# Shifted copies of V by block on GpSimd and VectorE, and a first product taken input by input: one change at the start of a Trainium2 kernel

## The chip, the cores and the metric

The kernel runs on one core of one Trainium2 chip. The time is the device time of one execution in microseconds (us), and smaller is better. A core has TensorE (PE in the profile, with its weight loads as PEld), VectorE (DVE), ScalarE (ACT), GpSimd (POOL) and SyncE (SP), an on-chip memory SBUF, an accumulation memory PSUM that TensorE writes, and 16 DMA engines. Each engine works through its own list of instructions in order. DMAs are issued by an engine, here mostly by POOL, and then run on their own.

## The reference

Sliding-window causal attention (8 batches, 8 heads, 576 positions, head size 64, window 64), followed by a two-layer feed-forward stage with a hard-swish between.

```python
rel = pos[:, None] - pos[None, :]
mask = (rel >= 0) & (rel < 64)
scores = np.where(mask, scale * np.matmul(q, k.transpose(0, 1, 3, 2)), -1e9)
attn = softmax(scores)                      # over the keys
x = np.matmul(attn, v)                      # then to (8*576, 512): 4608 tokens
h = x @ w_in                                # 512 -> 2048
g = h * np.clip(h + 3.0, 0.0, 6.0) / 6.0
out = g @ w_out                             # 2048 -> 512
```

Inputs and output are float32; the kernel computes in bfloat16 with float32 accumulation.

## The kernel before

**Tiling.** Heads go in pairs: a unit of attention is t = 4 * batch + pair, so T = 32 units. The feed-forward stage works on blocks of TB = 512 tokens, nine in all. Of a block, the first product gives 16 tiles hT of 128 features by 512 tokens (index fc), each the sum of four products, one for each pair of heads (`g` in L485: input g of the product is `xT[:, g]`). ACT and DVE then turn hT into gT (L494, L495). The second product gives four tiles of 128 tokens by 512 outputs, each the sum of 16 products (L518), in units of four.

**Order.** The order of instructions on each engine is the order of the program text; nothing is reordered (`manual_schedule`). Waits between engines follow from which tiles, and which parts of them, an instruction reads and writes. `moe` is a queue of feed-forward units, and `weave(n)` issues the next n of them among the attention of a later batch.

**Batch 0** has a path of its own. POOL issues its loads: q and k by pair (L107), then V (L126, five blocks of 128 positions, the last of 64), then the input weights in three parts (L163: a quarter, a quarter and a half of the columns, that is fc 0 to 3, 4 to 7 and 8 to 15), then fills that build the masks (`late_windows`, L196), the output weights in two halves (L169), and q, k and V of batch 1 (L118, L137). TensorE begins with products on zeros (`warm`, L656), turns q and k (`t_q`, `t_k`, L221) as they land and computes scores (`s0_`, L248 and L251), which ACT exponentiates.

The window of 64 lies across blocks of 128, so V is also needed shifted by 64 positions. `Vn[0]` holds batch 0's V by block, `Vs[0]` the shifted one: its upper half of block m is the lower half of Vn's block m, and its lower half of block m + 1 is the upper half of Vn's block m. `shift_early(g, move)` (L147) makes it for one pair of heads and all blocks in two copies. DVE does pairs 0 and 1 (L711, L712), ACT pairs 2 and 3 (L714, L715).

`pv_early(t)` (L354) multiplies the weights with Vn and Vs, and DVE divides by the sums (L363, L364) into `opg`. `x_early(t)` turns that on TensorE (L375, into a PSUM tile `xp`) and ACT copies it to `xT` (L378): this is input g of the first product. `begin(0, pools, between)` (L554, called at L726) starts the first product of block 0: for fc 0, 1 and 2 it issues inputs 0 to 2, then `x_early(3)`, then fc 3's inputs 0 to 2, and then input 3 of these four. The other 12 tiles follow from the queue, all four inputs at a time.

**PSUM** has eight banks: ps_t has three, ps_h two, ps_acc one, and ps_o one tile of two. A tile is held until its last reader has read it.

**Batch 1** follows from L775: two units of the second product, the turn of pair 4, two units, and then a loop over the four pairs, which issues the turn of the next pair, the scores and (L790) 2, 4 and 2 units of the second product.

The start of the program, in its order (excerpt):

```python
load_early_v()                                   # L678
for i in range(3):
    load_w_in(i)                                 # L680
late_windows()                                   # L681
load_w_out(0)
...
for g in range(2):
    shift_early(g, nc.vector.tensor_copy)        # L712
s0_(3)
for g in range(2, NG):
    shift_early(g, nc.scalar.copy)               # L715
```

Of the kernel before, what the change touches and what calls it, by code (L numbers as in the profile page):

```python
# [10 lines left out]
F32 = mybir.dt.float32  # L11
# [13 lines left out]
P = 128  # L25
D = 64
W = 64
# [9 lines left out]
def kernel(  # L37
# [9 lines left out]
    nc = tc.nc  # L47
    B, H, S, _ = q.shape
    DM, FF = moe_w_in.shape
    NT = B * S  # L50
    NG = H // 2
    SP = S // R
    NW = S // W
    NM = (S + P - 1) // P
    NFC = FF // P
    TB = 512
# [12 lines left out]
    ps_o = ctx.enter_context(tc.tile_pool(name="ps_o", bufs=1, space=PSUM))  # L69
    ps_t = ctx.enter_context(tc.tile_pool(name="ps_t", bufs=3, space=PSUM))  # L70
    ps_h = ctx.enter_context(tc.tile_pool(name="ps_h", bufs=2, space=PSUM))
    ps_acc = ctx.enter_context(tc.tile_pool(name="ps_acc", bufs=1, space=PSUM))
# [14 lines left out]
    Vn, Vs = ([t[:].rearrange("p (m h c) -> p m h c", m=NM, h=H) for t in Vflat[i::2]] for i in range(2))  # L87
# [56 lines left out]
            memset(t[:, :, :, 0:VO], 1.0)  # L144
            memset(t[:, :, :, VO + P : VW], 1.0)

    def shift_early(g, move):  # L147

        vn, vs = Vn[0], Vs[0]
        hs = slice(2 * g, 2 * g + 2)  # L150
        move(out=vs[W:P, :, hs], in_=vn[0:W, :, hs])
        move(out=vs[0:W, 1:NM, hs], in_=vn[W:P, 0 : NM - 1, hs])

    def shift(b):

# [4 lines left out]
    def load_w_in(i):  # L160
        n = FF // 4
        c = (slice(0, n), slice(n, 2 * n), slice(2 * n, FF))[i]
        nc.gpsimd.dma_start(  # L163
            out=win16[:, :, c], in_=moe_w_in[:, c].rearrange("(g p) f -> p g f", p=P)
        )
# [14 lines left out]
    zeros = consts.tile([P, TB], BF16, name="zeros")  # L180
# [20 lines left out]
    def late_windows():  # L201

        for part in halves:
            select(band, part, -1, 1, -1, 0.0)
            select(band, part, W, -1, 1, 0.0)
            select(first, part, 0, -1, 1, 0.0)
# [29 lines left out]
    def t_k(t):  # L236
        b, g = divmod(t, NG)
        tp = transposed_heads(ps_acc, staged[b][1], g)
        nc.vector.tensor_copy(
            out=KT[t % 4][:, W:].rearrange("q (p r) -> q p r", r=R),  # L240
            in_=tp[:].rearrange("q r p -> q p r"),
        )
# [96 lines left out]
    def pv_early(t):  # L339
        b, g = divmod(t, NG)  # L340
        vn, vs, pz, pl = Vn[b % 2], Vs[b % 2], Pz[t % 4], Pl[t % 4]
        if t in (1, 3):
            os = [ps_h.tile([P, 1, 512], F32, name="oh", tag="bk") for _ in range(2)]
        else:
            os = [ps_o.tile([P, 2, 512], F32, name="o", tag="o")]
        n = len(os)
        for h in range(2):
            hh = 2 * g + h
            o = os[h % n][:, h // n]
            for m in range(NM):  # L350
                om = o[:, m * (D + 1) : (m + 1) * (D + 1)]
                for a in range(2):
                    last = m == NM - 1
                    nc.tensor.matmul(  # L354
                        om[a * W : (a + 1) * W], lhsT=pl[:, h, a * W : (a + 1) * W] if last else pz[:, h, m, a, :],
                        rhs=(vn if a and not last else vs)[:, m, hh, 0 : D + 1], start=True, stop=True,
                    )
        opg = work.tile([P, NM, 2, D], BF16, name="opg")
        for i, o in enumerate(os):
            hs = slice(i, i + 2 // n)  # L360
            ov = o[:, :, 0 : NM * (D + 1)].rearrange("p h (m c) -> p h m c", c=D + 1)
            rec = recs[:, t, hs, 0:NM]
            nc.vector.reciprocal(out=rec.unsqueeze(3), in_=ov[:, :, :, D : D + 1])  # L363
            nc.vector.tensor_tensor(  # L364
                out=opg[:, :, hs].rearrange("p m h d -> p h m d"), in0=ov[:, :, :, 0:D],
                in1=rec.unsqueeze(3).to_broadcast([P, 2 // n, NM, D]), op=MULT,
            )
        opgs[t] = opg

    def x_early(t):  # L370
        b, g = divmod(t, NG)
        opg = opgs.pop(t)
        tp = ps_t.tile([P, NM, P], BF16, name="xp", tag="bk")
        for m in range(NM):
            nc.tensor.transpose(  # L375
                out=tp[:, m, :], in_=opg[:, m].rearrange("p h d -> p (h d)"), identity=ident[:]
            )
        nc.scalar.copy(out=xT[:, g, 0:S], in_=tp[:].rearrange("p m q -> p (m q)")[:, 0:S])  # L378
# [86 lines left out]
    halfway, units = {}, {}  # L465

    def first_units(kb):
        t0 = kb * TB % XR
        gT = gpool.tile([P, NFC, TB], BF16, name="gT")
        gTs[kb] = gT  # L470

        def unit(fc, part=2, pool=None):
            if part < 2 and fc in halfway:
                hT = halfway.pop(fc)
            else:
                if pool is None:
                    if late[0] == 0:
                        pool = (ps_h, ps_h, ps_t, ps_acc, ps_t, ps_t)[(fc - NG) % 6]
                    else:
                        pool = ps_t if late[0] == 1 or fc % 2 else ps_h  # L480
                hT = (
                    ps_o.tile([P, 2, 512], F32, name="hTo", tag="o")[:, 0] if pool is ps_o
                    else pool.tile([P, TB], F32, name="hT", tag="bk")[:]
                )
            for g in ((0, 1, 2), (3,), range(NG))[part]:  # L485
                nc.tensor.matmul(  # L486
                    hT, lhsT=win16[:, g, fc * P : (fc + 1) * P], rhs=xT[:, g, t0 : t0 + TB],
                    start=(g == 0), stop=(g == NG - 1),
                )
            if part == 0:  # L490
                halfway[fc] = hT
                return
            t1 = t1pool.tile([P, TB], BF16, name="t1")
            nc.scalar.activation(out=t1[:], in_=hT, func=RELU, bias=half_const[:], scale=1.0 / 6.0)  # L494
            nc.vector.scalar_tensor_tensor(  # L495
                out=gT[:, fc, :], in0=t1[:], scalar=1.0, in1=hT, op0=MIN, op1=MULT
            )

        units[kb] = unit
        return [lambda fc=fc: unit(fc) for fc in range(NFC)]  # L500
# [30 lines left out]
    moe = deque()  # L531
# [3 lines left out]
    def queue_block(kb, kept=2 * NG):  # L535

        f = first_units(kb)
        moe.extend(left[:2])
        del left[:2]
        n = len(left)  # L540
        for i, unit in enumerate(f):
            moe.extend(left[i * n // NFC : (i + 1) * n // NFC])
            moe.append(unit)
        left[:] = second_units(kb)
        n = len(left) - kept
        moe.extend(left[:n])
        del left[:n]
# [6 lines left out]
    def begin(kb, pools, between):  # L554

        def part(fc):
            moe.popleft()
            units[kb](fc, 0, pools[fc])

        for fc in range(3):  # L560
            part(fc)
        between()
        for fc in range(3, len(pools)):
            part(fc)
        for fc in range(len(pools)):
            units[kb](fc, 1)

    def weave(n):
        for _ in range(min(n, len(moe))):
            moe.popleft()()  # L570
# [82 lines left out]

    T = B * NG

    def warm(pool, n):  # L656

        wt = pool.tile([P, TB], F32, name="wt", tag="bk")
        for _ in range(n):
            nc.tensor.matmul(wt[:], lhsT=zeros[:, 0:P], rhs=zeros[:], start=True, stop=True)  # L660

    nc.vector.memset(zeros[:], 0.0)
    nc.vector.memset(ident[:], 0.0)
# [3 lines left out]
        out=ident[:], in_=ident[:], pattern=[[-1, P]], compare_op=mybir.AluOpType.not_equal,  # L667
# [8 lines left out]
    nc.vector.memset(first[:], 1.0)  # L676
    pads(1, nc.vector.memset)
    load_early_v()  # L678
    for i in range(3):
        load_w_in(i)  # L680
    late_windows()  # L681
    load_w_out(0)
    staged[1] = load_qk(1, 2)
# [3 lines left out]
    nc.vector.memset(recs[:], 1.0)  # L687
    zero_rows(1)
    nc.vector.memset(Pl[0][:], 1.0)
    nc.vector.memset(Vs[0][0:W, 0], 0.0)  # L690
    for t in Pl[1:]:
        nc.vector.memset(t[:], 1.0)
    nc.vector.memset(ones[:], 1.0)
# [2 lines left out]


    warm(ps_h, 12)
    t_k(0)
    t_q(0)  # L700
    t_k(1)
# [6 lines left out]
    t_k(3)  # L708
    t_q(3)
    s0_(2)  # L710
    for g in range(2):  # L711
        shift_early(g, nc.vector.tensor_copy)  # L712
    s0_(3)
    for g in range(2, NG):  # L714
        shift_early(g, nc.scalar.copy)  # L715
    warm(ps_acc, 6)
    pv_early(0)
    pv_early(1)
    warm(ps_acc, 2)
    x_early(0)  # L720
    pv_early(2)
    x_early(1)
    pv_early(3)
    x_early(2)
    queue_block(0, 0)
    begin(0, (ps_acc, ps_t, ps_t, ps_o), lambda: x_early(3))  # L726
    def group(t, n):

        if t >= 2 * NG:
# [35 lines left out]
    n = NG  # L765
# [12 lines left out]
    for t in range(n, n + 4):  # L778
        if t < n + 3:
            turn(t + 1)  # L780
        s = s_first(t, min(t + 1, n + 3))

        def copies():
            if t < n + 3:
                turned(t + 1, 0)
                turned(t + 1, 1)

        weights(t, s, s_rest(t), own, copies)
        if t < n + 3:
            weave((2, 4, 2)[t - n])  # L790
    nc.gpsimd.tensor_copy(out=seen[:], in_=P0[(n + 3) % 4][0:1, 0, 0, 0:1])
    staged[2] = load_qk(2, 1)
    for t in range(n, n + 4):
# [22 lines left out]
    for t in range(2 * NG, T):  # L816
        b, g = divmod(t, NG)
# [52 lines left out]
```

## Time and profile before

| | before |
|---|---|
| median of 3 runs | 324.89 us (324.28 to 325.29) |
| the profiled execution | 324.49 us |
| its span, first to last instruction | 322.8 us |
| TensorE busy | 307.5 us (95%) |
| DVE, ACT, POOL busy | 177.3, 187.4, 122.9 us |
| TensorE busy from 17.13 to 21.78 us | 3.82 of 4.65 us |
| TensorE busy from 21.78 to 25.35 us | 3.19 of 3.57 us |
| TensorE busy from 25.35 to 36.57 us | 11.22 of 11.22 us |

Times inside the profile count from the span's start. "Busy" is the time in which an engine has an instruction under way; waits, DMA issues apart, are not in it. The chain that ended last goes back from the last instruction, at each step to what released it. A timeline line gives start, duration, engine, line, operation, tiles (out<-in) and, in brackets, the idle time before it and what ended that. A line of the DMA view gives the tile, the issuing queue, how many, the size of one and the median time from issue to landing. "L495" is line 495 of the kernel.

### The profile page before, as it was taken

What the parts mean: (1) busy time and instruction counts of PE and PEld (TensorE: products, weight loads), DVE (VectorE), ACT (ScalarE), POOL (GpSimd) and SP (SyncE); (2) the same over time, 40 slices, a digit from 0 to 9 for tenths busy, and PEclk for the clock granted to TensorE, in tenths of its full rate; (3) what the DMA queues carried; (4) which work ended last, traced back from release to release, by engine and by line L of the source; (5) the groups of instructions that cost most, each with busy time, mean ns of one, the idle gap of its engine ahead of it and who ended that gap; (6) DMA issues with size and microseconds to landing.
All of it is one profiled execution on the core that took longest, in us unless ns stands there. A gap on an engine that the chain in (4) does not pass through costs nothing.

```text
span 322.8 us, 11140 instructions
## 1 busy us (share of the span) xinstructions
PE 307.5 (95%) x4822; PEld 155.5 (48%) x4822; DVE 177.3 (55%) x384; ACT 187.4 (58%) x349; POOL 122.9 (38%) x167
## 2 busy tenths in 40 slices
PE   6889999999999999999999999999999999999992
PEld 2744455445444555555555555555544444444440
DVE  7676647488446752775277626762666156334300
ACT  2768565598547764776477637773674256445310
POOL 8961204688775434563356335633331000000000
PEclk9999999999999999999999999999999999999997
DMA  6999994979979942993299338943012200110011
GB/s 92 161 211 207 207 181 110 214 105 115 197 104 164 125 116 88 162 131 111 80 163 129 115 100 139 152 102 94 17 51 52 85 32 0 60 40 34 34 70 69
DMA packets 57592, 35.67 MB, mean 111 GB/s; under 512 B 39872, under 2 KB 51648, under 8 KB 57536
## 3 DMA queue, kind: packets, MB, share of 16 engines
q0 software_dynamic: 35904, 18.81, 44.6%
q1 hardware_dynamic: 21632, 16.08, 19.2%
q8 instruction: 39, 0.64, 0.8%
q14 instruction: 17, 0.14, 0.1%
HBM read 37.62 MB, written 9.44 MB: 146 GB/s over the span
## 4 chain that ended last, share of the span: by engine, by line
PE 83%; DVE 4%; DMA 3%; ACT 3%; POOL 3%; issue 2%; SPq 0%; POOLq 0%; DVEq 0%; ACTq 0%
PE hT L486 36%; PE acc L518 35%; PE o L403 4%; PE s L310 2%; PE acco L518 2%; PE tk L276 2%; DMA V<-in_v_dram 2%; DMA xT<-opg 2%; POOL qk L107 2%; POOL V L126 1%; ACT t L494 1%; DVE gT L495 1%; DVE opg L364 1%; PE tq L276 1%; ACT e L323 0%
## 5 line engine op out<-in xcount | busy, mean ns | idle before, releaser
L495 DVE SCALAR_TENSOR_TENSOR gT<-t,hT 128x512 bf16<-128x512 bf16 x142 | 97.0, 688 | 84.8 <-ACT t L494 84.0
L486 PE MATMUL hT<-xT,win 128*128 128x512 bf16 x568 | 133.9, 379 | 1.7 <-DVE gT L495 0.6
L518 PE MATMUL acc<-wout,gT 128*128 128x512 bf16 x544 | 129.0, 379 | 0.6 <-ACT QZ L283 0.6
L494 ACT ACTIVATE t<-hT,half_const 128x512 bf16<-128x512 f32 x142 | 97.0, 689 | 52.8 <-PE hT L486 52.3
L486 PEld LDWEIGHTS <-win 128*128 128x128 bf16 x576 | 55.7, 98 | 68.4 <-issue 3.4
L518 PEld LDWEIGHTS <-gT 128*128 128x128 bf16 x576 | 54.3, 98 | 63.6 <-issue 0.9
L331 POOL TENSOR_TENSOR Pz<-e,band 128x512 bf16<-128x512 bf16 x48 | 54.2, 1146 | 0.0
L328 POOL TENSOR_TENSOR P<-e,first 64x256 bf16<-64x256 bf16 x24 | 15.9, 663 | 87.4 <-ACT e L319 87.4
L524 ACT COPY osb<-acc 128x512 f32<-128x512 f32 x34 | 19.9, 586 | 42.2 <-PE acc L518 36.2
L323 ACT ACTIVATE e<-s 128x512 bf16<-128x512 f32 x56 | 30.0, 590 | 0.0
L283 DVE COPY KT<-tk 128x576 bf16<-128x576 bf16 x28 | 20.8, 743 | 5.3 <-ACT e L319 4.5
L137 POOL DMA_DIRECT2D V<-in_v_dram x22 | 18.0, 821 | 11.8 <-DMA win<-in_moe_w_in_dram 5.9
L412 DVE TENSOR_REDUCE sums<-o 128x12 f32<-128x24 f32 x26 | 4.6, 178 | 27.4 <-PE o L403 27.4
L403 PEld LDWEIGHTS <-Pz 64*64 64x64 bf16 x1120 | 13.4, 108 | 12.8 <-issue 11.4
L426 DVE TENSOR_TENSOR opl<-o,recs 128x256 bf16<-128x256 f32 x52 | 19.2, 406 | 0.0
L283 ACT COPY QZ<-tq 128x576 bf16<-128x576 bf16 x28 | 17.8, 636 | 1.5 <-PE tq L276 1.5
L319 ACT ACTIVATE e<-tk 64x128 bf16<-64x128 f32 x28 | 7.6, 271 | 14.4 <-PE tq L296 14.4
L403 PE MATMUL o<-V,Pz 64*64 64x65 bf16 x1040 | 15.3, 195 | 0.0
L310 PE MATMUL s<-QZ,KT 64*64 64x64 bf16 x896 | 14.4, 195 | 0.4 <-DVE gT L495 0.4
L276 PE MATMUL tk<-ident,qk 64*64 64x64 bf16 x504 | 14.0, 195 | 0.0
L276 PE MATMUL tq<-ident,qk 64*64 64x64 bf16 x504 | 14.0, 195 | 0.0
L276 PEld LDWEIGHTS <-qk 64*64 64x64 bf16 x1008 | 11.6, 106 | 2.3 <-issue 2.1
(102 smaller groups left out, 204.9 us busy)
## 6 DMA issues: line engine op xcount, KB each, us to landing
out_dram<-osb SPq DMA_DIRECT2D x36, 256.0 KB, 2.3
V<-in_v_dram POOLq DMA_DIRECT2D x16, 256.0 KB, 5.8
V<-V SPq DMA_DIRECT2D x6, 432.0 KB, 4.7
qk<-in_k_dram POOLq DMA_DIRECT2D x4, 576.0 KB, 5.9
qk<-in_q_dram POOLq DMA_DIRECT2D x4, 576.0 KB, 9.0
wout<-in_moe_w_out_dram POOLq DMA_DIRECT2D x2, 1024.0 KB, 19.0
qk<-in_q_dram POOLq DMA_DIRECT2D x12, 144.0 KB, 4.3
qk<-in_k_dram POOLq DMA_DIRECT2D x12, 144.0 KB, 4.3
```

The costliest lines, as they stand in the source:

```text
L276: nc.tensor.transpose(out=hosts[t][z][halves[h], r * W : (r + 1) * W], in_=staged[b][halves[z], 2 * g + h, r * D : (r + 1) * D], identity= ...
L283: (nc.scalar.copy if z else nc.vector.tensor_copy)(out=(QZ[t % 4][:, 0] if z else KT[t % 4][:, W:]).rearrange("q (p r) -> q p r", r=RL), i ...
L310: nc.tensor.matmul(ss[h][halves[i], c, m, r], lhsT=keys(t, h, W * (w - 1), r), rhs=QZ[t % 4][halves[h], 0, w * W : (w + 1) * W], start=Tru ...
L323: nc.scalar.activation(out=e[:].rearrange("p c m r w -> p (c m r w)"), in_=ss[h][:].rearrange("p c m r w -> p (c m r w)"), func=EXP, scale ...
L331: muls[h].tensor_tensor(out=Pw[t % 4][:, h].rearrange("p c m r w -> p (c m) (r w)"), in0=e[:].rearrange("p c m r w -> p (c m) (r w)"), in1 ...
L403: nc.tensor.matmul(o[i][halves[c], c0 : c0 + D + 1], lhsT=p, rhs=vt[:, 2 * g + h, v0 : v0 + D + 1], start=(r == 0), stop=(r == 1), skip_gr ...
L426: nc.vector.tensor_tensor(out=opg[:, :, i], in0=ov[i][:, 2:6, 1 : D + 1].rearrange("p (m h) d -> p m h d", h=2), in1=rec[:, i, 2:6].rearra ...
L486: nc.tensor.matmul(hT, lhsT=win16[:, g, fc * P : (fc + 1) * P], rhs=xT[:, g, t0 : t0 + TB], start=(g == 0), stop=(g == NG - 1),)
L494: nc.scalar.activation(out=t1[:], in_=hT, func=RELU, bias=half_const[:], scale=1.0 / 6.0)
L495: nc.vector.scalar_tensor_tensor(out=gT[:, fc, :], in0=t1[:], scalar=1.0, in1=hT, op0=MIN, op1=MULT)
L518: nc.tensor.matmul(acc, lhsT=gT[:, fc, ts * P : (ts + 1) * P], rhs=wout16[:, fc, :], start=(fc == 0), stop=(fc == NFC - 1),)
L524: nc.scalar.copy(out=osb[:], in_=acc)
```

## The change

- `shift_early` takes a block m instead of a pair: the two copies of a block for all eight heads. POOL copies blocks 0 and 1, between its second and third load of the input weights; DVE copies blocks 2, 3 and 4 (the last has one copy only). ACT copies none. The fill of the first lower half of Vs moves ahead of POOL's copies.
- Block 0's first product begins with five tiles instead of four (fc 0 in ps_acc, 1 and 2 in ps_t, 3 and 4 in the two halves of the ps_o tile), input by input: input 0 of fc 0 to 2, then input 1 of these, inputs 0 and 1 of fc 3 and 4, input 2 of all five and input 3 of all five, with the turns of inputs 1 to 3 between. The banks of the other 11 tiles are assigned anew.
- Four products of 64 columns are added to the 12 on zeros at the start, and four instead of six stand ahead of pair 0.
- The loop of batch 1 issues 4, 2 and 2 units of the second product instead of 2, 4 and 2.

```diff
-    def shift_early(g, move):
+    def shift_early(m, move):
         vn, vs = Vn[0], Vs[0]
-        hs = slice(2 * g, 2 * g + 2)
-        move(out=vs[W:P, :, hs], in_=vn[0:W, :, hs])
-        move(out=vs[0:W, 1:NM, hs], in_=vn[W:P, 0 : NM - 1, hs])
+        move(out=vs[W:P, m], in_=vn[0:W, m])
+        if m + 1 < NM:
+            move(out=vs[0:W, m + 1], in_=vn[W:P, m])
...
-        def unit(fc, part=2, pool=None):
-            if part < 2 and fc in halfway:
+        def unit(fc, gs=range(NG), pool=None, to=None):
+            if fc in halfway:
                 hT = halfway.pop(fc)
+            elif to is not None:
+                hT = to
             else:
                 if pool is None:
                     if late[0] == 0:
-                        pool = (ps_h, ps_h, ps_t, ps_acc, ps_t, ps_t)[(fc - NG) % 6]
+                        pool = ps_acc if fc == 8 else ps_h if fc in (5, 6, 11, 12) else ps_t
...
-            for g in ((0, 1, 2), (3,), range(NG))[part]:
+            for g in gs:
...
-            if part == 0:
+            if gs[-1] < NG - 1:
                 halfway[fc] = hT
                 return
...
     load_early_v()
-    for i in range(3):
+    nc.vector.memset(Vs[0][0:W, 0], 0.0)
+    for i in range(2):
         load_w_in(i)
+    for m in range(2):
+        shift_early(m, nc.gpsimd.tensor_copy)
+    load_w_in(2)
     late_windows()
...
     warm(ps_h, 12)
+    warm(ps_h, 4, W)
...
-    for g in range(2):
-        shift_early(g, nc.vector.tensor_copy)
+    for m in range(2, NM):
+        shift_early(m, nc.vector.tensor_copy)
     s0_(3)
-    for g in range(2, NG):
-        shift_early(g, nc.scalar.copy)
-    warm(ps_acc, 6)
+    warm(ps_acc, 4)
     pv_early(0)
     pv_early(1)
     warm(ps_acc, 2)
     x_early(0)
     pv_early(2)
+    queue_block(0, 0)
+    u = units[0]
+
+    def inputs(gs, fcs, **to):
+        for fc in fcs:
+            u(fc, gs, **to)
+
+    u(0, (0,), ps_acc)
+    inputs((0,), (1, 2), pool=ps_t)
     x_early(1)
     pv_early(3)
     x_early(2)
-    queue_block(0, 0)
-    begin(0, (ps_acc, ps_t, ps_t, ps_o), lambda: x_early(3))
+    inputs((1,), range(3))
+    both = ps_o.tile([P, 2, 512], F32, name="hTo", tag="o")
+    for fc in (3, 4):
+        u(fc, (0, 1), to=both[:, fc - 3])
+    x_early(3)
+    inputs((2,), range(5))
+    inputs((3,), range(5))
+    for _ in range(5):
+        moe.popleft()
...
         if t < n + 3:
-            weave((2, 4, 2)[t - n])
+            weave((4, 2, 2)[t - n])
```

More of the change, by code (lines that the diff above doesn't have):

```diff
@@ L557, in part @@
             moe.popleft()
-            units[kb](fc, 0, pools[fc])
+            units[kb](fc, range(NG - 1), pools[fc])
         for fc in range(3):
@@ L565, in begin @@
         for fc in range(len(pools)):
-            units[kb](fc, 1)
+            units[kb](fc, (NG - 1,))
     def weave(n):
@@ L654, with warm @@
     T = B * NG
-    def warm(pool, n):
+    def warm(pool, n, cols=TB):
         wt = pool.tile([P, TB], F32, name="wt", tag="bk")
         for _ in range(n):
-            nc.tensor.matmul(wt[:], lhsT=zeros[:, 0:P], rhs=zeros[:], start=True, stop=True)
+            nc.tensor.matmul(wt[:, 0:cols], lhsT=zeros[:, 0:P], rhs=zeros[:, 0:cols], start=True, stop=True)
     nc.vector.memset(zeros[:], 0.0)
@@ L689 @@
     nc.vector.memset(Pl[0][:], 1.0)
-    nc.vector.memset(Vs[0][0:W, 0], 0.0)
     for t in Pl[1:]:
```

## The prediction

> **What bounds the kernel now.** I read the page's busy shares and its chain first, then the chain of waits from 10 to 27 us, then the instructions of that stretch engine by engine and the DMA issues. The page:
>
> ```profile
> PE 307.5 (95%) x4822; PEld 155.5 (48%) x4822; DVE 177.3 (55%) x384; ACT 187.4 (58%) x349; POOL 122.9 (38%) x167
> ...
> PE 83%; DVE 4%; DMA 3%; ACT 3%; POOL 3%; issue 2%; SPq 0%; POOLq 0%; DVEq 0%; ACTq 0%
> ```
>
> TensorE holds 83% of the chain; the other engines' 17% lie almost all before 27 us and around 51 to 54 us. So whatever lets TensorE begin the first product's gapless run sooner moves the end one for one, as long as no transfer comes too late. The chain of waits over the start:
>
> ```profile
> 10.98 5.17 DMA V<-in_v_dram
> ...
> 16.27 0.59 DVE V L151
> ...
> 16.88 0.31 DVE V L152
> ...
> 17.22 0.38 DVE V L151
> ...
> 17.63 0.46 DVE V L152
> ...
> 18.12 0.23 DVE recs L363
> ...
> 20.61 0.83 DVE opg L364
> ...
> 22.67 1.67 PE hT L486 x7
> ```
>
> The last block of V lands at 16.15; DVE copies until 18.09 and only then divides pair 0 (18.12); its four divisions run back to back to 22.69. The same stretch on TensorE, from the timeline:
>
> ```profile
> 15.74 1.46 PE L660 MATMUL wt<-zeros 128*128 128x512 bf16 x6
> ...
> 20.51 0.45 PE L375 MATMUL xp<-ident,opg 128*128 128x128 bf16 x5 [0.36 <-DVE opg L364]
> ...
> 22.67 1.67 PE L486 MATMUL hT<-xT,win 128*128 128x512 bf16 x7 [0.29 <-ACT xT L378]
> ...
> 26.21 10.52 PE L486 MATMUL hT<-xT,win 128*128 128x512 bf16 x48
> 36.57 1.89 PE L518 MATMUL acc<-wout,gT 128*128 128x512 bf16 x8
> ```
>
> From 25.35 TensorE runs without a gap: 52 products until the second product at 36.57, 11.22 / 52 = 0.2158 us each. I measure the change by when that second product starts.
>
> **Arrivals.** Issues and landings, from the DMA view of 7.4 to 11.6 us:
>
> ```profile
> V<-in_v_dram POOLq DMA_DIRECT2D x4, 128.0 KB, 5.6
> ...
> V<-in_v_dram POOLq DMA_DIRECT2D x1, 64.0 KB, 5.2
> ```
>
> With the issue starts (7.48, 8.4, 9.26, 10.1, 10.98) the blocks land at about 13.1, 14.0, 14.95, 15.95 and 16.15. DVE has nothing to do from 14.74 to 16.27 (its first copy takes all five blocks at once, and so waits for the last).
>
> **The change part by part.**
>
> 1. *Shifted copies.* Removed: four copies on DVE (0.58, 0.31, 0.38, 0.46: 1.82 with gaps, 16.27 to 18.09) and four on ACT (16.66 to 19.65). ACT's were hidden: its first copy of xT starts at 19.75, just after its transposes end at 19.70. Added: four copies of 64x576 on POOL (blocks 0 and 1) and five on DVE (blocks 2, 3, half of 4). DVE's price is the clean row of the same shape, 0.306, plus 0.03 between two: block 2's pair runs 15.05 to 15.7, block 3's 16.07 to 16.7, block 4's ends 17.05. Two of the four old copies were longer than the shape asks (0.58 beside 0.38, 0.46 beside 0.31), by 0.15 and 0.2; both span the end of a POOL DMA issue (16.66 and 17.94). One such hit by the moved issue makes it 17.25. Pair 0's product of weights and V needs block 4 at its ninth multiplication, so twelve at about 0.02, the last one's 0.20 and 0.06 of signalling follow: the first division starts at T0 = 17.53, or 17.73 with a hit. I take 17.6.
>
> 2. *POOL's copies* show in no row. Nearest rows: its memset of 128 elements at 0.205 against 0.10 for one (0.83 ns an element), its one-element copy at 0.178, and its two-input multiplications, 663 ns for 256 elements and 1146 for 512 (1.89 ns an element). So one copy lies between 0.178 + 575 x 0.00083 = 0.66 and 0.178 + 575 x 0.00189 = 1.26. A copy reads one operand, so I take 0.7, near the memset. POOL is free at 13.15: 13.2 to 14.6 and 14.6 to 16.0, earlier than DVE. At 1.26 they end at 18.25 and T0 would be 18.8.
>
> 3. *The third load of the input weights* is issued behind those copies, at 16.0 instead of 13.14; POOL's later issues move with it by about 2.9. The queue hides that: the second load lands only at 21.1 (12.4 + 8.7), and the third is served after it in both kernels and lands at about 26.7. Its first user, fc 8, comes at about 28.5 below. The cover goes if POOL issues after about 19. POOL's fills of the masks move too; their first user is at 42.
>
> 4. *Order of the first product.* Counted from T0 with durations of before. Division 0 and signal: 1.13 (18.12 to 19.25). Transposes until ACT starts 0.50, ACT 0.64, signal 0.04: first products at T0 + 2.31. Three products 0.65; transposes of input 1 at T0 + 2.96. Now fc 1 and 2 keep two of the three ps_t slots, so inputs 1, 2 and 3 share the third: input 2's transposes wait until ACT has copied input 1 (T0 + 4.09); pv_early(3) fills part of that and 0.5 of TensorE time is lost. This is the added wait; behind it stand all products. T0 + 4.13: transposes 0.29, three products 0.65, four for fc 3 and 4 0.86, transposes of input 3 at T0 + 5.93, 0.29 (division 3 ends near T0 + 4.95, no wait), then 10 + 44 products x 0.2158 = 11.65. The second product starts at T0 + 17.87. In before it is 36.57, so the break-even is T0 = 18.70. Input 3's copy ends at T0 + 7.06, just ahead of its first use at T0 + 7.30, so the old waits for inputs 2 and 3 are gone.
>
> 5. *Evictions.* Five tiles end within 1.1 us. ACT and DVE take 0.6 to 0.65 each in a row (28.88: five in 3.26), DVE is through fc 0 near 26.8 and fc 8 takes that bank at about 28.5. No wait.
>
> 6. *Small ones.* Four 64-column products more at the start: TensorE waits there for q and k until 5.58, and DVE is busy with fills until 6.83; nothing. Two 0.216 us idle products fewer before pair 0: the gap they leave is empty anyway. The Vs fill moves within DVE's fills; nothing.
>
> 7. *Four units instead of two at the first step of batch 1* delays the turn of pair 6 by 1.73. Its q lands at 42.85 (issued at 19.44, 23.4 to landing) and it runs at 43.27 in before; with a gain of 1.1 it would stand at 43.9, still after. Without it an earlier start would meet that landing. The second half of the output weights (landed at 17.94 + 21.7 = 39.6) is now needed at 41.43 + 1.83 - 1.1 = 42.2: no wait. Batch 1's V lands at 48.3 (33.66 + 14.6), its first use moves from 51.0 to about 49.9.
>
> **Sum.** 17.6 + 17.87 = 35.47 against 36.57: 1.1 us gained, carried to the end because TensorE is nearly the whole chain from 57 us on. The profiled execution took 324.49 (span 322.8 plus 1.7 around it) and would take 323.4; it is 0.4 below the median of 324.89, from which I forecast 323.8.
>
> **The lock.** In this trace POOL's multiplications stay at 1141 to 1157 ns and DVE's 0.69 us evictions beside them keep their length, but none of those DVE forms is a copy from SBUF to SBUF. The Trainium skill, SBUF — State Buffer, "Who interferes with whom", says that VectorE and GpSimd share one port pair as an exclusive lock and that the loser blocks. By that rule the sum would be about 0.5 smaller (the first rival, worked out below); the two lengthened copies above agree in kind, no row here shows it for POOL copies.
>
> **Rivals.**
>
> *DVE's and POOL's copies take turns (same).* One 0.7 copy and then the other's 0.31: POOL until 16.2, DVE's last four from 16.2 at 0.33, end 17.5, T0 about 18.0, with a hit 18.2; second product at 35.9 to 36.1, 0.5 to 0.7 gained: 324.3. For it: both work on the same two tiles in the same 1.1 us. Against: the rows that do not lengthen.
>
> *POOL's copies are slow and block DVE (slower).* With turns taken, the last copy ends at 13.2 + 4 x c + 1.5 and T0 is 0.48 later. At c = 1.26 that is 19.75 and 20.2, second product at 38.1: 1.5 lost, 326.4. It loses from c = 0.88 (T0 = 18.7) and by over 1 us from c = 1.13. Against: a copy has one operand, and fills ran at 0.83 ns.
>
> *The copies wait for all five blocks (slower).* Then POOL starts at 16.2, ends at 19.0, T0 = 19.5: 0.8 lost, 325.7. Against: hT starts at 21.78, before its tile's third load lands at 26.7, so loads are followed by part.
>
> *The start is hidden.* A transfer of batch 1 stops TensorE at 43 to 50 us and takes the gain back: 324.9. Against: margins of 1 us and more in 3 and 7.
>
> **How the numbers follow.** Below 0.3% (1.0 us) a measurement of this kernel can hardly tell a change. Forecast as above 0.47; taking turns 0.22; hidden 0.06; slow POOL copies 0.13; waits for all blocks or a bank held longer than I count 0.12. Of the last two nearly all is slower, about 0.01 within the bound. So faster 0.47, same 0.29, slower 0.24. Forecast's own range: T0 of 17.2 to 17.7, 323.3 to 323.9. The range for 8 in 10 goes from 323.1 to 325.8, which takes in turns and part of the slow cases.
>
> **What would show it.** POOL should show four 64x576 copies of about 0.7 between 13 and 16.2; DVE five of 0.31 ending near 17.1 to 17.3; recs L363 at about 17.6; a TensorE wait of about 0.5 before the transposes of input 2, released by ACT; no wait before fc 8; the second product at 35.5. Wrong if POOL's copies end after 18, if DVE's copies are longer than 0.5 (the lock), or if TensorE waits for a DMA at 28, 43 or 50.

## The result and the profile after

The changed kernel is slower: 326.8 us against 324.24 us (medians of 18 runs each), a ratio of 1.0077 with a 95% interval of 1.0055 to 1.0098. The forecast was 323.8 us and the range 323.1 to 325.8. One run of the changed kernel, of 330.92 us, fell in a slower state of the chip and is left out of the ratio.

The profiled execution took 327.83 us and its span is 326.1 us, so it is a little slower than the median. The waits of TensorE in the changed kernel between 14 and 60 us (who waited for what, in all, how often, the longest):

```profile
PE hTo L488 <- DVE gT L497: 2.6, 1, 2.6
PE o L354 <- DVE V L150: 0.9, 2, 0.5
PE ot L403 <- ACT e L319: 0.4, 1, 0.4
PE xp L375 <- DVE opg L364: 0.3, 1, 0.3
PE hT L488 <- ACT xT L378: 0.3, 1, 0.3
PE xp L375 <- ACT xT L378: 0.3, 1, 0.3
```

One wait of 2.6 us stands at the top, at a place where the prediction had none. Each of the others is 0.5 us or less. L488 is the first product, L497 the second step of its eviction on DVE. The timeline shows where it lies, first TensorE:

```profile
26.06 0.81 PE L488 MATMUL hT<-xT,win 128*128 128x512 bf16 x3
26.71 0.38 PE L488 MATMUL hTo<-xT,win 128*128 128x512 bf16 x1
29.73 0.38 PE L488 MATMUL hTo<-xT,win 128*128 128x512 bf16 x1 [2.64 <-DVE gT L497]
29.95 11.34 PE L488 MATMUL hT<-xT,win 128*128 128x512 bf16 x44
41.13 1.89 PE L520 MATMUL acc<-wout,gT 128*128 128x512 bf16 x8
```

and then DVE:

```profile
27.20 1.88 DVE L497 SCALAR_TENSOR_TENSOR gT<-t,hT 128x512 bf16<-128x512 bf16 x3 [3.33 <-ACT t L496]
29.00 0.68 DVE L497 SCALAR_TENSOR_TENSOR gT<-t,hTo 128x512 bf16<-128x512 bf16 x1
```

The product at 26.71 is the last one of fc 3, that at 29.73 the last one of fc 4. Both write `hTo`, the ps_o tile of two banks. Between them in the program stands the eviction of fc 3, which DVE ends at 29.68, after those of fc 0, 1 and 2. Without the wait fc 4's product would have followed at 26.93: it is 2.80 us late.

The 44 products behind it take 11.2 us and not 44 x 0.2158 = 9.5. The windows of the stretch show why (length, busy time and count of PE, PEld, DVE, ACT and POOL, then the granted clock, the DMA share and GB/s):

```profile
27.10:29.73 2.63, 0.00 (x0) 0.00 (x0) 2.48 (x4) 1.80 (x4) 0.88 (x1) 1.00 1.25 208
29.73:30.95 1.22, 1.22 (x5) 0.51 (x5) 0.09 (x1) 0.69 (x1) 0.00 (x0) 0.86 1.23 207
30.95:34.10 3.15, 3.15 (x9) 1.19 (x8) 1.67 (x3) 1.37 (x2) 0.71 (x1) 0.51 1.22 205
34.10:41.13 7.03, 7.03 (x35) 3.14 (x34) 5.13 (x8) 5.47 (x8) 1.68 (x6) 1.00 1.25 205
```

TensorE does nothing for 2.63 us, starts again at full clock, and then the granted clock falls to about a half. The second row's 0.86 is a mean: 0.87 us at 1.00 and 0.35 us at 0.51 give it, so the fall comes about 0.9 us after the restart, near 30.60. From there to about 34.03 the clock is 0.50 in the mean, 3.4 us in all. TensorE counts as busy all the while, with products 0.427 us apart (that spacing is read from the weight loads, for instance 32.27, 32.70, 33.12).

The second product starts at 41.13; it started at 36.57 before. Of these 4.56 us the end shows 3.3 (spans of 326.1 and 322.8). The rest comes back between 84 and 112 us: the profile of before has three TensorE waits there, 0.7 us for nothing that the profile shows, 0.5 us for a DMA into xT and 0.6 us for ACT, and the changed kernel has one of 0.9 us. From the second product to the end the profiles of this study take 284.4 to 286.4 us, so the end of a single profile can't show a difference under 2 us; the stretch itself can, and the medians can down to about 1 us.

### The profile page after: what moved, and what is told of

It reads as the page before. It is cut to its first block, busy times and chain, and to the rows that moved or that the text cites. A ratio compares the mean times of both kernels' runs of the same rounds, so it can differ in the third digit from the quotient of the medians.

```text
span 326.1 us, 11140 instructions
## 1 busy us (share of the span) xinstructions
PE 309.5 (95%) x4824; PEld 156.4 (48%) x4824; DVE 178.3 (55%) x385; ACT 184.7 (57%) x345; POOL 125.2 (38%) x171
## 4 chain that ended last, share of the span: by engine, by line
PE 86%; ACT 3%; DVE 3%; POOL 2%; DMA 2%; issue 2%; POOLq 0%; ACTq 0%
PE hT L488 37%; PE acc L520 36%; PE o L403 4%; PE s L310 2%; PE acco L520 2%; DMA V<-in_v_dram 2%; PE tk L276 2%; DVE gT L497 2%; POOL qk L107 1%; ACT t L496 1%; PE tq L276 1%; POOL V L126 1%; PE hTo L488 1%; PE xp L375 0%; ACT e L323 0%
## 5 line engine op out<-in xcount | busy, mean ns | idle before, releaser
L497 DVE SCALAR_TENSOR_TENSOR gT<-t,hT 128x512 bf16<-128x512 bf16 x141 | 96.6, 688 | 86.5 <-ACT t L496 86.0
L488 PE MATMUL hT<-xT,win 128*128 128x512 bf16 x564 | 134.9, 383 | 2.0 <-issue 0.9
L488 PEld LDWEIGHTS <-win 128*128 128x128 bf16 x576 | 56.2, 98 | 72.2 <-issue 8.3
L283 ACT COPY QZ<-tq 128x576 bf16<-128x576 bf16 x28 | 17.8, 637 | 1.5 <-PE tq L276 1.5
```

The lines of the kernel that those rows point to most:

```text
L283: (nc.scalar.copy if z else nc.vector.tensor_copy)(out=(QZ[t % 4][:, 0] if z else KT[t % 4][:, W:]).rearrange("q (p r) -> q p r", r=RL), i ...
L488: nc.tensor.matmul(hT, lhsT=win16[:, g, fc * P : (fc + 1) * P], rhs=xT[:, g, t0 : t0 + TB], start=(g == 0), stop=(g == NG - 1),)
L497: nc.vector.scalar_tensor_tensor(out=gT[:, fc, :], in0=t1[:], scalar=1.0, in1=hT, op0=MIN, op1=MULT)
```

## The experiments

A measure that does not depend on when V happens to land is the time from the first division (recs L363 on DVE) to the second product: 36.57 - 18.12 = 18.45 us in before and 41.13 - 18.79 = 22.34 us after. The prediction's sum has 17.87 us.

My theory after the two profiles: fc 4's last product waits for fc 3's eviction because both lie in one tile ("one tile"), and the idle time of that wait then costs half the clock ("clock"). The rivals: five tiles that end together are too much for ACT and DVE in any case; the shifted copies, or what is issued later because of them, carry part of the loss.

### e1: both last products ahead of the evictions

```diff
-            if gs[-1] < NG - 1:
+            if hold or gs and gs[-1] < NG - 1:
...
-    inputs((3,), range(5))
+    inputs((3,), range(3))
+    inputs((3,), (3, 4), hold=True)     # products only
+    inputs((), (3, 4))                  # then both evictions
```

> The changed kernel, but the last products of fc 3 and fc 4 are issued one after the other, and both tiles are evicted only then. One tile (the 2.64 us wait at 27.09 exists because fc 3 and fc 4 lie in one ps_o tile, so that fc 4's last product waits for the evictions of fc 3 that stand ahead of it): no wait over 0.3 us between 25 us and the second product, products 0.216 us apart throughout, second product at the last landing of V + 19.4 (36.7 if V lands at 17.29, 35.5 if at 16.15 as in before); time 326.8 - 4.3 = 322.5, up to 323.8 if later stretches give back less than they took. Rival, evictions: ACT and DVE can't clear five tiles that end together, TensorE waits over 1.5 us for a bank at another tile, time 325.3 to 326.8.

Measured: 323.44 us against 324.52, ratio 0.9972 (0.9946 to 0.9997). The wait is gone, and no other has come:

```profile
26.29 0.59 PE L488 MATMUL hTo<-xT,win 128*128 128x512 bf16 x2
26.73 9.66 PE L488 MATMUL hT<-xT,win 128*128 128x512 bf16 x44
36.22 1.89 PE L520 MATMUL acc<-wout,gT 128*128 128x512 bf16 x7
```

The second product starts 36.22 - 18.37 = 17.85 us after the first division, 4.49 us less than in the changed kernel, and the granted clock is 1.00 throughout. ACT and DVE clear five tiles without holding TensorE up, so the rival falls. The time is within the expected 322.5 to 323.8.

### e2: fc 4 in a bank of its own

```diff
-                        pool = ps_acc if fc == 8 else ps_h if fc in (5, 6, 11, 12) else ps_t
+                        pool = ps_acc if fc == 7 else ps_h if fc in (5, 10, 11, 15) else ps_t
...
-    for fc in (3, 4):
-        u(fc, (0, 1), to=both[:, fc - 3])
+    u(3, (0, 1), to=both[:, 0])
+    u(4, (0, 1), ps_h)
```

> The changed kernel, but fc 4 has a ps_h bank of its own (and later tiles are dealt so that none waits); the order of products and evictions stays. One tile: the wait at fc 4's last product is gone without any change of order; second product at V's landing + 19.4 to 19.8, time 322.5 to 323.9. Rival, order: the wait comes from the order of evictions and products alone; it stays at 2.6 us, time 326.8.

Measured: 323.47 us against 324.52, ratio 0.9974 (0.9947 to 1.0001). Products and evictions stand in the order of the changed kernel, and the wait is gone all the same:

```profile
26.16 0.38 PE L488 MATMUL hTo<-xT,win 128*128 128x512 bf16 x1
26.38 9.88 PE L488 MATMUL hT<-xT,win 128*128 128x512 bf16 x45
```

The second product comes 36.09 - 18.24 = 17.85 us after the first division. Together with e1: the wait needs both the shared tile and an eviction of one half that stands ahead of a product into the other half. The halves are different banks, so nothing in the data asks for it. Whether the wait is put in when the program is built or arises on the chip, no run here shows.

### e3, e9, e10: the gap filled, wholly and in part

```diff
-    inputs((3,), range(5))
+    inputs((3,), range(4))
+    warm(ps_h, 12)                      # e9: 3, e10: 6
+    inputs((3,), (4,))
```

> The changed kernel with 12 products on zeros (2.6 us) between the last product of fc 3 and that of fc 4. Clock (the products after the wait are 0.427 us apart for 3.2 us because TensorE stood idle for 2.64 us): the wait for fc 3's eviction stays, fc 4's last product starts at about the same time, but the products behind it are 0.216 apart at once; second product 1.7 us earlier than in the changed kernel (V's landing + 22.1 instead of + 23.84), time 325.1 to 325.6. Rival (the slow products have another cause, the evictions or the memory): still 0.427 apart, 326.8.

> As e3_gap_filled, with 3 products on zeros instead of 12: 0.65 us of the wait filled, about 2.0 us idle left. Clock: if an idle stretch of 2.0 us is enough, products behind it are 0.427 apart for about 3 us and the second product comes 22.3 us after the first division; if not, 20.65.

> As e3_gap_filled, with 6 products on zeros: 1.3 us filled, about 1.35 us idle left, less than the 1.6 us that before shows at 6.3 to 7.9 us with no slower products behind it. Clock: no slow products, second product 20.65 us after the first division. Rival (any break in this place costs the clock): 22.3.

In e3 the wait stays (DVE ends the eviction of fc 3 at 29.00) and TensorE spends it on products on zeros:

```profile
26.24 2.75 PE L662 MATMUL wt<-zeros 128*128 128x512 bf16 x12
29.05 0.38 PE L488 MATMUL hTo<-xT,win 128*128 128x512 bf16 x1
29.27 9.66 PE L488 MATMUL hT<-xT,win 128*128 128x512 bf16 x43
38.76 1.46 PE L520 MATMUL acc<-wout,gT 128*128 128x512 bf16 x6
```

The products behind it are at full speed; the second product comes 38.76 - 18.11 = 20.65 us after the first division, 1.69 us sooner than in the changed kernel. That is the clock's share, and 20.65 - 17.85 = 2.80 is the wait's. The time is 326.33 us against 324.52, ratio 1.0057 (1.0022 to 1.0092): still slower than before, and above the 325.1 to 325.6 that I expected. The ratios of e3 and of the changed kernel (1.0077) differ by less than their intervals, so the clock's share is shown by the profiles of the stretch and not by the times.

e9 and e10 leave 2.00 and 1.35 us of idle time in the same place; e9:

```profile
29.22 0.38 PE L488 MATMUL hTo<-xT,win 128*128 128x512 bf16 x1 [2.00 <-DVE gT L497]
```

Neither has slow products: both come to 20.66 us (38.93 - 18.27 and 38.76 - 18.10). (Each ran once: 326.14 and 325.06 us, with before at 323.34.) So here 2.0 us of idle TensorE cost no clock and 2.64 us did, in both kernels that have that gap (the changed one and e5). At its start e7 has a wait of 2.06 us, for a load of k, and the clock stays at 1.00 there too. Each gap rests on one profiled execution of one kernel, that of 2.64 us on two, so where between 2.06 and 2.64 us the cost begins, and whether it always begins there, is open.

### e4: the shifted copies alone

```diff
 # the kernel before, with
-    for g in range(2):
-        shift_early(g, nc.vector.tensor_copy)
+    for m in range(2, NM):
+        shift_early(m, nc.vector.tensor_copy)
     s0_(3)
-    for g in range(2, NG):
-        shift_early(g, nc.scalar.copy)
...
 # and blocks 0 and 1 on POOL, between the loads of the input weights
```

> The kernel before with only the copies changed (blocks 0 and 1 on POOL, 2 to 4 on DVE, the third input-weight load behind POOL's copies); first product as before, with four tiles. Copies help: the first division comes 1.5 us after V's landing instead of 1.97, the divisions and the second product move by the same 0.45, 324.24 - 0.45 = 323.8. Turns: DVE copies that meet a POOL copy take 0.5 to 0.7, but those are over before the last landing, so the gain is the same; if POOL's copies end after the landing, no gain and up to 0.5 lost, 324.2 to 324.7.

Measured: 324.48 us against 324.52, ratio 1.0002 (0.9976 to 1.0028). No gain shows, though the interval of about 0.8 us either way could not tell the expected 0.45 from nothing; the profile can. POOL's copies cost 0.66 each, but DVE's are no longer the 0.31 of before. DVE in e4:

```profile
14.90 0.66 DVE L150 COPY V<-V 64x576 bf16<-64x576 bf16 x1 [0.27 <-DMA V<-in_v_dram]
15.59 0.69 DVE L152 COPY V<-V 64x576 bf16<-64x576 bf16 x1
16.31 0.60 DVE L150 COPY V<-V 64x576 bf16<-64x576 bf16 x1
16.94 0.37 DVE L152 COPY V<-V 64x576 bf16<-64x576 bf16 x1
17.34 0.33 DVE L150 COPY V<-V 64x576 bf16<-64x576 bf16 x1
18.14 0.22 DVE L363 RECIPROCAL recs<-o 128x10 f32<-128x10 f32 x1 [0.47 <-PE o L354]
```

and POOL in e4:

```profile
14.73 0.66 POOL L150 COPY V<-V 64x576 bf16<-64x576 bf16 x1
15.45 0.66 POOL L152 COPY V<-V 64x576 bf16<-64x576 bf16 x1
16.06 0.75 POOL L163 DMA_DIRECT2D win<-in_moe_w_in_dram  x1
```

A DVE copy that meets a POOL copy ends 0.15 to 0.17 us after it (15.56 and 15.39; 16.28 and 16.11), whenever it began, while POOL's stay at 0.66. The third copy overlaps POOL's next DMA issue in the same way and ends 0.10 us after it (16.91 and 16.81). DVE's five take 2.77 us instead of 1.65, and the first division comes at 18.14, where it was at 18.12 before, with block 2 of V landing at 14.80 (about 14.95 before). From there to the second product it is 36.60 - 18.14 = 18.46 us, as before.

### e5: the new first product alone

The changed kernel with `shift_early` by pair again, as in before (DVE and ACT, all loads of the input weights issued at once, six products on zeros ahead of pair 0).

> The changed kernel with the copies as before (by pair, DVE and ACT, all input weights issued at once, six products on zeros ahead of pair 0): the new first product alone. One tile: the wait of 2.6 us at fc 4's last product and the slow products behind it are all there, second product 22.2 us after the first division; the copies alone were worth 0 (1.0002), so the time is that of the changed kernel, 326.3 to 327.0, ratio to before 1.006 to 1.009. Rival (the shifted copies, or the later issue behind them, carry part of the loss): under 325.7.

Measured: 328.32 us against 324.22, ratio 1.0101 (1.0062 to 1.0141). The whole loss is there without any of the new copies:

```profile
29.04 0.38 PE L488 MATMUL hTo<-xT,win 128*128 128x512 bf16 x1 [2.64 <-DVE gT L497]
40.43 1.89 PE L520 MATMUL acc<-wout,gT 128*128 128x512 bf16 x8
```

40.43 - 18.09 = 22.34 us, the changed kernel's figure. The time is 1.3 us above the 326.3 to 327.0 that I expected; its profile has a TensorE wait of 1.79 us for ACT before 105.89, which the changed kernel's has not, and why it is there is open.

### e6, e8: fewer copies on POOL

Both are e1 with the copies dealt otherwise: in e6 DVE makes all nine, in e8 POOL makes block 0 only.

```diff
-    for m in range(2):
-        shift_early(m, nc.gpsimd.tensor_copy)
+    shift_early(0, nc.gpsimd.tensor_copy)        # e8; e6 has no such line
...
-    for m in range(2, NM):
+    for m in range(1, NM):                       # e8; e6: range(NM)
         shift_early(m, nc.vector.tensor_copy)
```

> As e1_products_first, but DVE does all nine copies, POOL none. Lock (DVE copies of 0.60 to 0.69 instead of 0.31 are those that meet a POOL copy): all nine take 0.31 to 0.33, except where a POOL DMA issue ends (0.45). Nine at 0.34 from 14.8, the last three after V's landing: first division at 18.1 to 18.4, second product at 36.0 to 36.3, time as e1, 323.2 to 323.7. Rival (the long copies are long by themselves, by their partitions or beside the DMAs): some of blocks 2 and 3 still take 0.6 to 0.69, first division after 18.8, 324 or more.

> As e1_products_first, but POOL copies block 0 only (done by about 14.7, before DVE is free) and DVE blocks 1 to 4. Lock: DVE's seven copies take 0.31 to 0.33 each, the last ends about 1.0 after V's landing, the first division comes at 17.5 to 17.8 (18.37 in e1), second product at 35.4 to 35.7 (36.22), time 0.6 below e1, 322.8. Rival (no lock): the first division stays within 0.2 us of e1's, time as e1.

DVE's copies in e6, summed up (minimum, median and maximum ns):

```profile
L150 DVE COPY V<-V x5: 298/305/743, 14.8 to 17.9; 64x576 bf16<-64x576 bf16 x5
```

The longest of them, and what POOL does beside it, from the timeline:

```profile
15.83 0.91 POOL L169 DMA_DIRECT2D wout<-in_moe_w_out_dram  x1
16.10 0.74 DVE L150 COPY V<-V 64x576 bf16<-64x576 bf16 x1
```

With the four of L152 (0.30 to 0.31 in the timeline), eight of the nine take 0.30 or 0.31. The ninth is under way while POOL issues the output weights (15.83 to 16.74) and ends 0.10 us after that. So it is POOL's copies and DMA issues that lengthen DVE's copies, and not their shape. Not all work on POOL does: four of e6's copies, from 14.75 to 16.06, ran beside POOL's fills of the masks (L196, 13.85 to 15.88) and took 0.30 or 0.31. The Trainium skill, SBUF — State Buffer, "Who interferes with whom", states that VectorE and GpSimd share one port pair as an exclusive lock, and counts a copy on VectorE among the operations that can contend for it. The runs agree for copies that meet a POOL copy (0.54 to 0.69 when begun 0.37 us or more before its end, 0.31 alone); beside the fills they show no such waiting (0.37 at most, in e4 from 16.94). In e8 the copies take 0.30 to 0.52.

The first division came earlier in neither (18.65 and 18.56; e1 has 18.37), against the 18.1 to 18.4 and 17.5 to 17.8 that I expected. DVE waits for V in neither. In e6 it copies without a break from 14.75 to 18.18: nine copies, one of them lengthened, take that long. In e8 it starts on the copies only at 15.46, because its work on the last pair before them begins at 14.78 (14.17 in e1); the chain of waits goes back from there to a load of k that lets TensorE turn at 11.63 (11.02 in e1). Whether the dealing of e8 is the better one, with that load on time, is therefore open. Their times are e6 323.26 us, ratio 0.9985 (0.9955 to 1.0014), and e8 322.94 us, ratio 0.9961 (0.9932 to 0.9990), both against 324.22. From the first division to the second product both take 17.85 us. e8 is the fastest kernel of the study, faster than before and after; that it beats e1 is not shown.

### e7: the old order of batch 1

```diff
-            weave((4, 2, 2)[t - n])
+            weave((2, 4, 2)[t - n])
```

> As e1_products_first, but with 2, 4 and 2 units of the second product in batch 1's loop as in before. If the landing of pair 6's q (42.85 in before) matters: the turn of pair 6 would run at about 42.9 and waits up to 0.5 us there, time up to 0.5 above e1 (323.4 to 323.9). If not: no wait on a DMA between 40 and 50, time as e1.

Measured, on e1 as base: 323.23 us against 324.22, ratio 0.9974 (0.9941 to 1.0008), the same as e1. Pair 6's q lands at 42.98 (issued at 22.28, 20.7 to landing) and its turn runs from 42.88 to 43.5; its second product starts 0.16 us after its first, where the turn before shows none, so the landing holds it for about 0.15 us at most. The new order of units neither helped nor hurt at this start.

## Why the prediction was wrong

The error is in step 5, "Evictions", which ends in "No wait", and in the rivals, none of which worked it out (the chances name "a bank held longer than I count", without a place or a price). I followed each tile to the product that would take its *bank* next and found none late. I did not ask what else reads or writes the same *tile*. fc 3 and fc 4 are the two halves of one ps_o tile, and a product into one half was held until the eviction of the other half, which stands ahead of it in the program, had ended. The old first product put one tile into ps_o and left the second half unused. The change's own diff shows the shared tile (`both`), so the question could have been asked: by the prediction's own figures, with the evictions as they were measured, fc 4's last product stands at T0 + 8.2 and DVE is through fc 3 near T0 + 10.9 (fc 0's last product ends at T0 + 7.7, ACT takes 0.69, DVE 2.49 for four). That difference, 2.7 us, is the wait (2.64 measured).

The 5.66 us between the predicted second product (35.47) and the measured one (41.13) come to:

- 1.19 from the first division, at 18.79 and not 17.6. V's last block but one landed at 17.29, and 16.15 was the last landing of before; from landing to division it was 1.50 where the sum had 1.45. V's landing differs between executions: by the chains of waits block 2 lands at 14.80 in e4, 15.05 in e1 and 15.83 in e7, which issue the same loads as the changed kernel, and by the DMA view at about 14.95 in before. So the late landing is not put down to the change.
- 2.80 from the wait at fc 4 (e1 and e2 take it away, e3 keeps it).
- 1.69 from the clock behind it (e3, e9 and e10). No step had a term for it, since it follows from a wait that step 5 put at nothing.
- The order itself took 0.02 less than the sum had.

The steps one by one:

- *Step 1, the copies.* T0 of 17.6 assumed that POOL and DVE don't disturb each other. They take turns: the first rival, which put T0 at 18.0 to 18.2 for V as it landed in before. e4 has 18.14 and e3 18.11. The copies alone bring the first division no earlier (e4, 18.14 against 18.12, time 1.0002), where the step had 0.5 us. The rows of before that spoke against it were multiplications on POOL beside evictions on DVE; none was a copy between two places in SBUF.
- *Step 2, POOL's copy.* 0.7 taken, 0.66 measured; the slow-copy rival is out.
- *Step 3, the late issue.* The third load of the input weights was issued at 16.38 and nothing waited for it.
- *Step 4, the order.* 17.87 us from the first division to the second product predicted, 17.85 measured in every kernel in which the wait is gone and TensorE is not held otherwise (e1, e2, e6, e7, e8). The added wait for input 1's copy is there, with 0.3 us where the step had 0.5. This part of the change is right: it is worth 18.45 - 17.85 = 0.6 us by itself.
- *Step 6.* The idle products and fills cost nothing that the profiles show.
- *Step 7, the order of batch 1.* No wait came. With the old order e7's turn does meet the landing of q, as the step said, but it costs about 0.15 us at most.
- *One for one to the end.* Not shown to better than 1 us. The medians of e1 and after differ by 1.05% of 324.3, 3.4 us with an uncertainty of about 1.1 (the two half-widths, 0.0026 and 0.0022, added as squares), for 4.5 us at the second product.

So the direction was right for a kernel that was not the one measured: without the wait the change gains 0.9 us (e1, 0.9972; its interval goes from 0.1 to 1.8 us), and with it, it loses 2.5. That 0.9 lies near the forecast 1.1 is in part luck: of the two parts of that sum the order's 0.6 was there and the copies' 0.5 was not.

## What to carry to other kernels

When two results share one tile, a write into one part can be made to wait for readers of the other part that stand ahead of it in the program; ask for each tile, not only for each bank, who reads it between two of its writes, or issue all writes of the shared tile before its first reader. A wait on TensorE can cost more than its length, so price an idle stretch as long as this one (2.64 us) with slow products behind it. Copies moved from DVE to POOL were no second pair of hands here, while both copied within SBUF.

## What the runs showed of the hardware

- After 2.64 us without a product TensorE's granted clock fell to 0.50, not at once but 0.9 us after it had begun to work again (1.1 us in e5), and stayed there for 3.4 us (1.69 us lost). After 2.00 and 1.35 us, in the same place, it stayed at 1.00.
- A DVE copy of 64x576 from SBUF to SBUF took 0.31 us alone. When it began 0.37 us or more before the end of a POOL copy of the same shape it took 0.54 to 0.69 us and ended 0.15 to 0.17 us after that one, which stayed at 0.66. POOL's DMA issues lengthened it too (0.74 in e6); POOL's fills hardly did (0.30 and 0.31 in e6, 0.37 at most in e4).
- A POOL copy of 64x576 bf16 takes 0.66 us and starts 0.72 us after the one before it.
